# A fused attention and gated feed-forward kernel: the first q/k load cut in two, and a new order for every engine

## The chip, the cores and the metric

The kernel runs on one core of one Trainium2 chip. Its time is the device time of one execution in microseconds (us). Times of one instruction are given in nanoseconds (ns) where that is plainer. TensorE (PE in the rows) multiplies matrices, VectorE (DVE), ScalarE (ACT) and GpSimd (POOL) do the element-wise work, and SyncE (SP) issues the transfers.

## The reference, cut to what matters

Causal attention over 4 batches, 12 heads, 448 positions and 64 dimensions per head, and then a feed-forward part (768 to 1024 to 768) with a convolution of three taps over the positions and a gate:

```
scores = mask(q @ k.T / 8);  attn = softmax(scores);  x = attn @ v      # per head
h = relu(x @ w_in)                                                      # 768 -> 1024
c = conv_w[0]*h[s-1] + conv_w[1]*h[s] + conv_w[2]*h[s+1]
out = (h * sigmoid(c)) @ w_out                                          # 1024 -> 768
```

## The kernel before, in words

**Attention.** Two heads make a pair; there are 6 pairs in each of 4 batches, so 24 pairs, numbered g. For each pair SP loads `raw` (k and q, transposed, 128 partitions of 2 x 448 numbers) and `vraw` (the values). TensorE computes the scores (L453) in blocks of 64 queries. A block k needs keys 0 to 64(k+1) alone, and the blocks are taken in the order 6, 5, 1, 3, 4, 2, 0. For the first two batches the scores are two steps, (6, 5, 1) and (3, 4, 2, 0); for the last two they are one. VectorE adds the mask and finds the row maximum (L488), ScalarE takes the exponential and its sum (L494), TensorE transposes the result (L553), ScalarE or VectorE copies the transposes out of PSUM (L562), and TensorE multiplies them by the values (L583). In batch 0 the division by the sum comes last, and TensorE spreads the reciprocals over the rows (L599); in the others ScalarE or VectorE divides before the transposes (L525).

**Feed-forward.** Numbers are cut into a high and a low part (`parts`, `wih`, `wil`, `woh`, `wol`), and a product is three matmuls of 128 x 128 by 448 columns: L899 for `w_in` of batches 0 and 1, L779 for a joint form of batches 2 and 3 with sums of weights, L957 for `w_out`: 1116 in all. Between the two, `activate` does relu (L915), taps, gate and the cut into parts. The weights are loaded in 32 pieces of 384 columns (L361) and converted by a chain on ACT, DVE and POOL (L365, L368, L326/L325/L329, L340). The finished rows are stored by SP (L971).

**What sets the order.** Nothing is written in its final order. `plan.add` records steps: an engine (or several to choose from), a cost in ns, what the step needs and makes, and which buffers it takes and frees. `Plan.run` then goes through the open steps, always issues the one with the lowest rank, and moves that engine's clock on by the step's cost. A rank is the time at which the step could start, plus a lateness, plus a number from the table `OFFSET`. `SWITCH` is the cost that the planner adds when TensorE goes from one kind of step to another (0 products, 1 scores, 2 values, 3 transposes), and `FROM` the time at which it lets an engine begin. So each engine's order, and the choice between engines, comes out of these numbers; on the chip each engine runs its own list strictly in that order and waits on semaphores.

TensorE begins with eight matmuls on zeros (`idle`, L301), which write a bank that nothing reads, and two more such fills (4 and 7 matmuls) stand near the first pairs. PSUM's eight banks are three rings: `S` (four, for scores), `PT` (two, for transposes and values) and `acc` (two, for products).

Of the kernel before, what the change touches and what calls it, by code (L numbers as in the profile page):

```python
# [8 lines left out]
F32 = mybir.dt.float32  # L9
# [14 lines left out]
class Plan:  # L24
# [11 lines left out]
    FROM = {"PE": 3800.0, "SP": 500.0, "ACT": 3500.0}  # L36
    ISSUE = {}
    OFFSET = {
        "PT": {10: -100, 11: 250, 14: -500, 15: -11650, 18: -11650, 19: 200, 20: -150, 21: -100, 6: -7550},
        "after": {5: 9100},  # L40
        "c12": {0: 1950},
        "c22": {1: 550, 2: 6050, 3: 19800},
        "chain": {114: 6500, 142: 9650, 187: 20000, 197: 1800, 206: 7100, 215: 9600, 231: 7300, 29: 3150, 61: 7000},
        "cw": {0: 350},
        "exp": {0: -400, 1: 100, 11: 300, 12: 2650, 14: -100, 16: -6850, 17: -2150, 18: -18750, 20: -3000, 21: -8700, 22: -50,
            23: 450, 4: -9450, 5: 600},
        "g": {(0, 1): -250, (1, 1): 150, (1, 2): 300, (1, 5): -50, (1, 7): -50, (2, 1): -150, (2, 2): 200, (2, 3): 150, (3,
            1): -200, (3, 4): 9800, (3, 5): 16500},
        "least": {10: -450, 15: -2000, 16: -6900, 17: -500, 21: 450, 4: 150, 5: 150, 9: -250},
# [11 lines left out]
        "raw": {3: -12900, 4: 250, 5: 3750, 8: 550, 9: -1150},  # L61
        "rb": {1: -4300, 3: -15800},
        "s2": {1: 150, 2: -300, 3: -100},
        "s3": {0: -16000, 3: 100},
        "s4": {0: 150, 1: 100, 3: 14550},
        "scores": {16: -20000, 18: -14750, 4: 100, 5: 100, 6: -4750},
        "sum": {(1, 0): 950, (1, 1): -500, (1, 3): 150, (2, 2): -6650, (2, 3): -100, (3, 1): 1450, (3, 3): -6050},
        "t1": {2: -450},
        "t3": {0: -10350, 1: 150},
        "t4f": {0: 2700, 1: 450},  # L70
        "u2": {0: 700},
        "vraw": {1: 650, 2: 150, 22: 5000, 3: -850, 4: 3800, 5: 650, 7: 250},
# [4 lines left out]
    }  # L77
    SWITCH = {(0, 1): 90, (0, 2): 90, (3, 1): 90, (3, 2): 90, (1, 2): 95, (2, 1): 95, (1, 0): 200, (2, 0): 200, (1, 3): 100, (2, 3): 100, (0, 3): 20}
# [11 lines left out]
    def at(self, key):  # L90
        return self.slot[key]
# [119 lines left out]
def attn_ffn_kernel(ctx: ExitStack, tc: tile.TileContext, qk, v, w_in, conv_w, w_out, out):  # L211
# [8 lines left out]
    nc = tc.nc  # L220
    P = 128
# [11 lines left out]
    RANK = (6, 5, 1, 4, 3, 0, 2)  # L233

# [68 lines left out]
    def setup():  # L303
        nc.gpsimd.memset(bank_zeros, 0.0)
        idle(bank[7], 8)
# [105 lines left out]
    def pair(b, hp):  # L411
# [8 lines left out]
        def load():  # L420
            nc.sync.dma_start(out=at(raw), in_=qk[b, hp])

        def load_v():
            nc.sync.dma_start(out=at(vraw).rearrange("p c j d -> p c (j d)"), in_=v[b, hp])

        plan.add(
            "SP", 1130, load, needs=after, makes=[raw], late=0,
            take=[("xg" if near else "raw", raw, lambda pool: pool.tile([P, 2, S], F32, name="raw", tag="xg"))],
        )
# [17 lines left out]
        def scores(blocks):  # L447
            for k in blocks:
                s, o = place(k)
                for j in range(2):  # L450
                    t = at(raw)[half(j)]
                    for k0, k1, to in [(128, 192, o), (0, 128, o + 64)] if k == 2 else [(0, KEYS[k], o)]:
                        nc.tensor.matmul(  # L453
                            at(s)[half(j ^ (k in SWAPPED)), to : to + k1 - k0], lhsT=t[:, 1, 64 * k : 64 * k + 64],
                            rhs=t[:, 0, k0:k1], start=True, stop=True,
                        )
# [597 lines left out]
```

## Time and profile before

| | us |
|---|---|
| median of 3 runs (lowest, highest) | 374.61 (374.46, 375.0) |
| the profiled execution, its time | 374.62 |
| the profiled execution, its span | 372.8 |

The span goes from the first instruction to the last. The execution's time is 1.8 us longer, which lies around the span; the profiled execution is within 0.01 us of the median.

### The profile page before, as it was taken

How to read it: one execution, taken by the hardware profiler on the slowest of the kernel's cores; microseconds unless marked ns; L12 is line 12 of the kernel's file. 1: busy time of each engine (PE TensorE's matmuls, PEld its weight loads, DVE VectorE, ACT ScalarE, POOL GpSimd, SP SyncE). 2: the span in 40 equal slices, each digit the busy share in tenths (PEclk: the TensorE clock that was granted, in tenths of full speed). 3: DMA queues.
4: the chain of work that ended last, by engine and by line, in shares of the span. 5: the costliest groups of instructions: out<-in, count | busy, mean ns of one | idle time of the engine just before them, and what ended most of it. 6: DMA issues, size and time to landing. Idle time of an engine off the chain costs nothing.

```text
span 372.8 us, 8941 instructions
## 1 busy us (share of the span) xinstructions
PE 364.5 (98%) x3367; PEld 305.5 (82%) x3367; DVE 265.0 (71%) x739; ACT 258.9 (69%) x708; POOL 164.4 (44%) x201
## 2 busy tenths in 40 slices
PE   8999998999999899999999999999999999999996
PEld 4777776988888697898988887887899999999995
DVE  4788897977874837866896868558999897742500
ACT  4899899899999556886769866879656147523211
POOL 2067774466553220324348887861211822521400
PEclk9999999999999999999999999999999999999999
DMA  7996414325575332501122253120000000111011
GB/s 272 401 358 207 168 44 143 86 81 167 146 242 172 118 120 88 159 11 37 49 86 87 72 152 111 61 62 26 1 2 0 2 0 0 52 49 49 2 74 74
DMA packets 15162, 37.54 MB, mean 101 GB/s; under 512 B 1808, under 2 KB 4880, under 8 KB 15120
## 3 DMA queue, kind: packets, MB, share of 16 engines
q1 hardware_dynamic: 15120, 36.99, 29.8%
q8 instruction: 26, 0.43, 0.5%
q14 instruction: 16, 0.13, 0.1%
HBM read 31.47 MB, written 5.51 MB: 99 GB/s over the span
## 4 chain that ended last, share of the span: by engine, by line
PE 86%; ACT 5%; DVE 4%; issue 2%; DMA 1%; POOL 1%; SPq 0%; ACTq 0%; DVEq 0%; POOLq 0%
PE bank L957 30%; PE bank L899 14%; PE bank L779 11%; PE bank L553 10%; PE bank L583 10%; PE bank L453 9%; ACT p L494 2%; DMA wraw<-in_w_out_dram 1%; PE bank L599 1%; PE bank L301 1%; ACT p L525 1%; DVE u L676 1%; DVE top L676 1%; DVE keep L676 0%; ACT u L968 0%
## 5 line engine op out<-in xcount | busy, mean ns | idle before, releaser
L957 PE MATMUL bank<-parts,woh 128*128 128x448 f32 x384 | 113.9, 371 | 0.0
L494 ACT ACTIVATE p<-bank,negm 128x320 f32<-128x320 f32 (+6 forms) x168 | 78.1, 483 | 17.2 <-DVE negm L488 16.1
L957 PEld LDWEIGHTS bank<-parts,woh 128*128 128x128 f32 x384 | 71.5, 188 | 5.4
L488 DVE CUSTOM_DVE_ANT_0 bank<-bank,mask 128x384 f32<-128x384 f32 (+6 forms) x168 | 66.2, 454 | 11.4 <-PE bank L453 11.3
L957 PE MATMUL bank<-parts,wol 128*128 128x448 f32 x192 | 71.5, 372 | 0.0
L340 POOL TENSOR_TENSOR parts<-u,parts 128x448 fp32r<-128x448 f32 x38 | 45.9, 1212 | 39.5 <-ACT parts L325 38.0
L899 PE MATMUL bank<-parts,wih 128*128 128x448 f32 x192 | 57.2, 376 | 0.5 <-ACT hr L915 0.5
L922 DVE SCALAR_TENSOR_TENSOR u<-hr,cw,u 128x448 f32<-128x448 f32 x64 | 46.8, 739 | 9.6 <-ACT u L935 8.9
L553 PE MATMUL bank<-ident,p 128*128 128x128 f32 x336 | 51.0, 278 | 2.6 <-DVE u L646 1.3
L553 PEld LDWEIGHTS bank<-ident,p 128*128 128x128 f32 x336 | 38.4, 140 | 11.8 <-ACT parts L325 1.6
L453 PE MATMUL bank<-raw 64*64 64x128 f32 (+5 forms) x768 | 46.0, 359 | 0.0
L583 PEld LDWEIGHTS bank<-pt,vraw 64*64 64x64 f32 x960 | 30.8, 133 | 15.8 <-issue 7.4
L583 PE MATMUL bank<-pt,vraw 64*64 64x64 f32 (+3 forms) x960 | 43.2, 317 | 0.1
L779 PE MATMUL bank<-parts,wih 128*128 128x448 f32 x150 | 42.9, 367 | 0.3 <-DVE hr L810 0.3
L525 ACT ACTIVATE p<-p,rcp 128x448 f32<-128x448 f32 (+6 forms) x90 | 40.8, 511 | 1.6 <-DVE rcp L513 1.5
L562 ACT COPY pt<-bank 128x512 f32<-128x512 f32 (+1 forms) x61 | 32.5, 550 | 12.7 <-PE bank L553 11.9
L329 POOL TENSOR_SCALAR parts<-u 128x448 fp32r<-128x448 f32 x20 | 11.9, 597 | 66.2 <-DVE u L928 50.4
L453 PEld LDWEIGHTS bank<-raw 64*64 64x64 f32 x768 | 29.5, 134 | 13.9 <-issue 7.6
L899 PEld LDWEIGHTS bank<-parts,wih 128*128 128x128 f32 x192 | 34.8, 188 | 4.2 <-ACT hr L915 0.9
L957 PEld LDWEIGHTS bank<-parts,wol 128*128 128x128 f32 x192 | 36.1, 188 | 2.5
L899 PE MATMUL bank<-parts,wil 128*128 128x448 f32 x96 | 35.9, 374 | 0.0
L494 ACT ACTIVATION_READ_ACCUMULATOR p<-bank,negm 128x1 f32 x168 | 35.8, 213 | 0.0
(91 smaller groups left out, 544.1 us busy)
## 6 DMA issues: line engine op xcount, KB each, us to landing
raw<-in_qk_dram SPq DMA_DIRECT2D x24, 448.0 KB, 4.1
vraw<-in_v_dram SPq DMA_DIRECT2D x24, 320.0 KB, 3.6
wraw<-in_w_in_dram SPq DMA_DIRECT2D x16, 383.8 KB, 7.0
wraw<-in_w_out_dram SPq DMA_DIRECT2D x16, 383.8 KB, 3.2
out_dram<-u SPq DMA_DIRECT2D x24, 224.0 KB, 1.9
wraw<-in_conv_w_dram SPq DMA_DIRECT2D x1, 23.8 KB, 5.9
```

Source lines behind the costliest of these rows:

```text
L340: engine.tensor_tensor(out=out(), in0=src(), in1=f32(hi()), op=ALU.subtract)
L453: nc.tensor.matmul(at(s)[half(j ^ (k in SWAPPED)), to : to + k1 - k0], lhsT=t[:, 1, 64 * k : 64 * k + 64], rhs=t[:, 0, k0:k1], start=True, ...
L488: nc.vector.tensor_tensor_reduce(out=t, in0=t, in1=mask[:, S - 64 : S - 64 + n] if k == 2 else mask[:, S - n : S], scale=-0.125, scalar=3. ...
L494: nc.scalar.activation(at(t)[:, h : h + n], at(s)[:, o : o + n], AF.Exp, bias=negm[g % 2][:, c : c + 1], scale=-1.0, accum_out=ssum[g % 2] ...
L525: mul(t, t, rcp[g % 2][:, c : c + 1])
L553: nc.tensor.matmul(to, lhsT=p, rhs=ident, is_transpose=True)
L562: copy(at(part)[:, o : o + n], at(pt)[:, :n])
L583: nc.tensor.matmul(at((pv, r))[half(j), q0:q1], lhsT=at(vraw)[half(r), c if c < 3 else 3 + (c - 3) // 2, j], rhs=t[half(r), :, j], start=c ...
L779: nc.tensor.matmul(at(bank)[:, :S], lhsT=weights(w)[:, c], rhs=at(operands[c])[:, part], start=q == 0, stop=q == len(prods) - 1,)
L899: nc.tensor.matmul(at(ph)[:, :S], lhsT=block(w, NCC * f + cc), rhs=at(x)[:, part], start=q == 0, stop=q == len(prods) - 1)
L922: nc.vector.scalar_tensor_tensor(out=t, in0=src, scalar=w, in1=t, op0=ALU.mult, op1=ALU.add)
L957: nc.tensor.matmul(at(po)[:, :S], lhsT=block(w, NF * m + f), rhs=at(g)[:, part], start=q == 0, stop=q == len(prods) - 1)
```

## The change

It has four parts.

1. The queries of every pair lie in memory in the order 6, 5, 1, 3, 4, 2, 0, and the first pair's `raw` is loaded by two transfers: columns 0 to 640 (all keys and the queries of blocks 6, 5 and 1), then the other 256. The first score step needs the first of them alone. All other pairs are loaded in one transfer as before.
2. TensorE begins with five matmuls on zeros in place of eight.
3. The planner's costs of TensorE's steps, of the exponential and of relu are other numbers, the switches between kinds are other numbers, the values are a kind of their own (mode 2), and TensorE's start is 2900 in place of 3800.
4. Every entry of `OFFSET` is another.

The work is the same: as many score, transpose, value, spread and product matmuls, on as many columns.

```diff
-    FROM = {"PE": 3800.0, "SP": 500.0, "ACT": 3500.0}
+    FROM = {"PE": 2900.0, "SP": 500.0, "ACT": 3500.0}
...
-        "PT": {10: -100, 11: 250, 14: -500, 15: -11650, 18: -11650, 19: 200, 20: -150, 21: -100, 6: -7550},
+        "PT": {10: -50, 17: -250, 19: -100, 23: -50, 4: -150, 5: -350, 6: -400},
...
-    SWITCH = {(0, 1): 90, (0, 2): 90, (3, 1): 90, (3, 2): 90, (1, 2): 95, (2, 1): 95, (1, 0): 200, (2, 0): 200, (1, 3): 100, (2, 3): 100, (0, 3): 20}
+    SWITCH = {(0, 1): 178, (0, 2): 170, (0, 3): 85, (1, 0): 95, (1, 2): 10, (1, 3): 95, (2, 0): 213, (2, 1): 103, (2, 3): 110, (3, 1): 167, (3, 2): 167, (3, 3): 120}
...
+    QUERIES = (6, 5, 1, 3, 4, 2, 0)
+    FIRST = S + 64 * 3
...
-        idle(bank[7], 8)
+        idle(bank[7], 5)
...
-        plan.add(
-            "SP", 1130, load, needs=after, makes=[raw], late=0,
...
+        cuts = (0, FIRST, 2 * S) if g == 0 else (0, 2 * S)
+        for z in range(len(cuts) - 1):
+            plan.add(
+                "SP", 1130 if g else (300, 830)[z], lambda z=z: load(cuts[z], cuts[z + 1]), needs=after, makes=[raw, (raw, z)], late=0,
...
-                "PE", 1650, lambda: scores((6, 5, 1, 3, 4, 2, 0)), makes=[("scores", g, 0), ("scores", g, 1)], drop=[raw],
+                "PE", 1573, lambda: scores((6, 5, 1, 3, 4, 2, 0)), makes=[("scores", g, 0), ("scores", g, 1)], drop=[raw],
...
-                    "PE", 830, lambda blocks=blocks: scores(blocks), makes=[("scores", g, i)], drop=[raw], mode=1,
+                    "PE", (930, 870)[i] if g else (1500, 980)[i], lambda blocks=blocks: scores(blocks), makes=[("scores", g, i)], drop=[raw], mode=1,
...
-                    "ACT", 237 + 0.83 * n, expo, needs=[("least", g, s)] + ([("exp", ("p", g, home))] if h else []), early=84,
+                    "ACT", 245 + 0.83 * n, expo, needs=[("least", g, s)] + ([("exp", ("p", g, home))] if h else []), early=84,
...
-                "PE", 110 * n // P, transp, slack=SLACK if b else 0, mode=3,
+                "PE", 109.3 * n // P - 75, transp, slack=SLACK if b else 0, mode=3, early=-75,
...
-            "PE", 170, lambda: spread(0), needs=[("r1", g, 0)], makes=[("rb", g, 0)], mode=1, take=[("S", rb)]
+            "PE", 400, lambda: spread(0), needs=[("r1", g, 0)], makes=[("rb", g, 0)], mode=1, take=[("S", rb)]
...
-            "PE", 1800, product, needs=[("pt", g, 0), ("pt", g, 1), vraw, ("rb", g, 0)], makes=[(pv, 1)], mode=1,
+            "PE", 2073, product, needs=[("pt", g, 0), ("pt", g, 1), vraw, ("rb", g, 0)], makes=[(pv, 1)], mode=2,
...
-            "PE", 1560, times_v, needs=[("pt", g, 0), ("pt", g, 1), vraw, *gate], makes=[(pv, 1)], mode=1,
+            "PE", 1473, times_v, needs=[("pt", g, 0), ("pt", g, 1), vraw, *gate], makes=[(pv, 1)], mode=2,
...
-        plan.add("ACT", 436, relu, needs=needs, makes=[(hr, 1)], take=[] if ph == hr else [("hr", hr)], drop=[] if ph == hr else [ph], late=0)
+        plan.add("ACT", 480, relu, needs=needs, makes=[(hr, 1)], take=[] if ph == hr else [("hr", hr)], drop=[] if ph == hr else [ph], late=0)
...
-    qk = _np.stack([k, q], axis=2).transpose(0, 1, 4, 2, 3)
+    queries = _np.concatenate([q[:, :, 64 * n : 64 * n + 64] for n in (6, 5, 1, 3, 4, 2, 0)], axis=2)
+    qk = _np.stack([k, queries], axis=2).transpose(0, 1, 4, 2, 3)
```

All cost numbers in the diff are the planner's own; how long something takes on the chip stands in the rows further down. Lines of the changed kernel are three to seven further on (L453 is L459, L553 is L559, L583 is L589, L779 is L785, L361 is L364, L971 is L977).

**Three places in the order.** First, SP's queue at the very start, before:

```order
L421 DMA raw<-in_qk_dram 128x896 x2
L424 DMA vraw<-in_v_dram 128x640
L421 DMA raw<-in_qk_dram 128x896
L361 DMA wraw<-in_conv_w_dram 128x95
L424 DMA vraw<-in_v_dram 128x640
```

and in the changed kernel:

```order
L425 DMA raw<-in_qk_dram 128x640
L425 DMA raw<-in_qk_dram 128x256
L425 DMA raw<-in_qk_dram 128x896
L428 DMA vraw<-in_v_dram 128x640
L425 DMA raw<-in_qk_dram 128x896
L364 DMA wraw<-in_conv_w_dram 128x95
```

The first pair's 896 columns have become 640 and 256, and each later transfer stands one place further back.

Second, TensorE at the last transposes of the attention (L553, L559; `p` are the exponentials of the last pair), where only products of the joint form (L779, L785) remain to be done afterwards; before, from the last products ahead of them to the values product (L583):

```order
L779 MATMUL bank_142<-parts,wil_83 128x448
L553 MATMUL bank_140<-ident,p_1_235 128x128
L553 MATMUL bank_140<-ident,p_1_237 128x2x64
L553 MATMUL bank_140<-ident,p_0_238 128x2x64
L553 MATMUL bank_140<-ident,p_1_240 128x128
L553 MATMUL bank_139<-ident,p_1_233 128x2x64
L553 MATMUL bank_139<-ident,p_1_240 128x128
L553 MATMUL bank_139<-ident,p_1_235 128x128
L553 MATMUL bank_139<-ident,p_1_237 128x2x64
L553 MATMUL bank_140<-ident,p_1_240 128x128
L553 MATMUL bank_140<-ident,p_1_237 128x2x64
L583 MATMUL bank_139<-pt,vraw_230 64x384 x2
```

and in the changed kernel, after the four transposes of the first bank:

```order
L785 MATMUL bank_142<-parts,wil_84 128x448
L559 MATMUL bank_140<-ident,p_1_233 128x2x64
L559 MATMUL bank_140<-ident,p_1_240 128x128
L559 MATMUL bank_140<-ident,p_1_235 128x128
L559 MATMUL bank_140<-ident,p_1_237 128x2x64
L785 MATMUL bank_142<-parts,wih_68 128x448 x2
L559 MATMUL bank_139<-ident,p_1_240 128x128
L559 MATMUL bank_139<-ident,p_1_237 128x2x64
L785 MATMUL bank_142<-parts,wil_84 128x448
L785 MATMUL bank_141<-parts,wih_69 128x448 x2
L589 MATMUL bank_140<-pt,vraw_231 64x384 x2
```

The ten transposes in one piece have become four, four and two with one and two products between them, and three products stand between the last transposes and the values.

Third, SP's queue where the first finished rows are stored (`out_dram`) and the last pieces of `w_out` are still to be loaded, before:

```order
L971 DMA out_dram<-u_249 128x448
L361 DMA wraw<-in_w_out_dram 128x1535 x2
L421 DMA raw<-in_qk_dram 128x896
L424 DMA vraw_231<-in_v_dram 128x640
L361 DMA wraw<-in_w_out_dram 128x1535
L971 DMA out_dram<-u_249 128x448
L361 DMA wraw<-in_w_out_dram 128x1535
L424 DMA vraw_230<-in_v_dram 128x640
L421 DMA raw<-in_qk_dram 128x896
L361 DMA wraw<-in_w_out_dram 128x1535 x2
```

and in the changed kernel:

```order
L364 DMA wraw<-in_w_out_dram 128x1535
L425 DMA raw<-in_qk_dram 128x896
L364 DMA wraw<-in_w_out_dram 128x1535
L977 DMA out_dram<-u_249 128x448
L364 DMA wraw<-in_w_out_dram 128x1535 x2
L977 DMA out_dram<-u_249 128x448
L364 DMA wraw<-in_w_out_dram 128x1535 x2
```

Before, six of the sixteen pieces of `w_out` stand behind the first store and three of them behind the second; in the changed kernel four stand behind the first and two behind the second, and no load of a pair stands among them.

## Rows read from the trace of the kernel before

**Rows 1.** The page, part 1: busy us, share of the span, instructions.

```profile
PE 364.5 (98%) x3367; PEld 305.5 (82%) x3367; DVE 265.0 (71%) x739; ACT 258.9 (69%) x708; POOL 164.4 (44%) x201
```

**Rows 2.** Stretches: length, then PE, PEld, DVE, ACT, POOL busy, clock, DMA.

```profile
12.00:60.00 48.00, 47.03 (x717) 34.05 (x712) 39.77 (x135) 44.41 (x138) 30.11 (x36) 1.00 0.63 221
60.00:120.00 60.00, 59.76 (x571) 50.40 (x572) 45.75 (x126) 57.09 (x159) 32.34 (x38) 1.00 0.47 143
```

**Rows 3.** The chain of waits, its last long piece: start us, us, what.

```profile
310.94 58.38 PE bank L957 x288
```

**Rows 4.** Timeline of the start: start us, us, engine, line, instruction, idle before.

```profile
1.19 2.74 PE L301 MATMUL bank<-zeros 128*128 128x384 bf16 x8 [1.19 <-POOL zeros L304]
3.88 0.31 PEld L453 LDWEIGHTS bank<-raw 64*64 64x64 f32 x8 [0.64 <-DMA raw<-in_qk_dram]
5.69 0.57 DVE L488 CUSTOM_DVE_ANT_0 bank<-bank,mask 128x384 f32<-128x384 f32 x1 [3.97 <-PE bank L453]
7.02 0.63 ACT L494 ACTIVATE p<-bank,negm 128x448 f32<-128x448 f32 x1 [4.80 <-DVE negm L488]
7.08 0.82 PE L301 MATMUL bank<-zeros 128*128 128x384 bf16 x4
```

**Rows 5.** Transfers from 1 to 4.25 us: GB/s in 40 equal slices.

```profile
GB/s 0 0 0 0 0 0 0 0 132 132 221 88 176 132 265 176 221 309 353 309 397 353 397 397 397 441 397 397 309 397 353 353 353 265 441 265 397 441 265 485
```

**Rows 6.** Timeline of TensorE where kinds of work meet.

```profile
172.78 1.76 PE L583 MATMUL bank<-pt,vraw 64*64 64x384 f32 x40
174.36 1.74 PE L453 MATMUL bank<-raw 64*64 64x448 f32 x32
176.03 1.09 PE L553 MATMUL bank<-ident,p 128*128 128x128 f32 x8
...
252.06 1.76 PE L583 MATMUL bank<-pt,vraw 64*64 64x384 f32 x40
253.75 0.67 PE L957 MATMUL bank<-parts,woh 128*128 128x448 f32 x2
...
125.09 0.45 PE L957 MATMUL bank<-parts,woh 128*128 128x448 f32 x1
...
125.88 1.79 PE L453 MATMUL bank<-raw 64*64 64x448 f32 x32
```

**Rows 7.** Timeline of TensorE where a pair's scores come in two parts.

```profile
37.30 1.09 PE L453 MATMUL bank<-raw 64*64 64x448 f32 x12
38.33 1.09 PE L553 MATMUL bank<-ident,p 128*128 128x128 f32 x8
39.35 1.03 PE L453 MATMUL bank<-raw 64*64 64x256 f32 x20
40.32 0.47 PE L899 MATMUL bank<-parts,wih 128*128 128x448 f32 x1
```

**Rows 8.** Timeline of TensorE from 57 to 61 us.

```profile
57.44 0.45 PE L899 MATMUL bank<-parts,wil 128*128 128x448 f32 x1
...
58.97 0.69 PE L899 MATMUL bank<-parts,wih 128*128 128x448 f32 x2 [0.48 <-ACT hr L915]
...
60.24 0.66 PE L553 MATMUL bank<-ident,p 128*128 128x128 f32 x4 [0.39 <-ACT p L525]
```

**Rows 9.** Timeline of TensorE and VectorE from 120 to 124 us.

```profile
121.09 0.65 PE L957 MATMUL bank<-parts,woh 128*128 128x448 f32 x2
...
123.44 0.63 PE L553 MATMUL bank<-ident,p 128*128 128x128 f32 x4 [1.29 <-DVE u L646]
...
120.78 0.39 DVE L365 TENSOR_SCALAR top<-wraw 128x384 f16<-128x384 bf16 x1 [1.37 <-DMA wraw<-in_w_out_dram]
```

**Rows 10.** The chain of waits from 84 to 146 us: its one transfer.

```profile
115.75 5.01 DMA wraw<-in_w_out_dram
```

**Rows 11.** Timeline of TensorE at the last pair's transposes and values.

```profile
258.71 1.09 PE L553 MATMUL bank<-ident,p 128*128 128x128 f32 x8
...
260.53 2.15 PE L583 MATMUL bank<-pt,vraw 64*64 64x384 f32 x40
...
262.62 0.68 PE L779 MATMUL bank<-parts,wih 128*128 128x448 f32 x2
```

More of the change, by code (lines that the diff above doesn't have):

```diff
@@ new lines @@
+        "PT": {10: -50, 17: -250, 19: -100, 23: -50, 4: -150, 5: -350, 6: -400},
+        "c12": {0: 4800, 2: -1250},
+        "c21": {2: 300},
+        "c22": {2: 9550},
+        "chain": {10: 800, 103: 10100, 152: 4050, 187: 20000, 198: 1250, 215: 4100, 23: 1300, 231: 11950, 3: 1450, 34: 300,
+            36: 1250, 39: 2550, 69: 1700},
+        "exp": {11: 1050, 12: -9700, 14: -100, 16: -100, 18: 100, 2: -50, 20: -2550},
+        "g": {(0, 1): -200, (1, 3): 150, (1, 5): -100, (2, 0): -200, (2, 1): -150, (2, 3): 50, (2, 5): 50, (3, 2): 450, (3,
+            4): 16550, (3, 5): 18800, (3, 7): 19950},
@@ new lines @@
+        "least": {0: -250, 10: 1100, 13: 1200, 14: 1000, 15: -50, 17: -11000, 18: -450, 19: -650, 2: 150, 20: 1150, 21: -1200,
[10 rows of a table added]
+        "raw": {0: -700, 9: 2850},
+        "rb": {1: 2000, 2: -7300},
+        "s1": {0: -1850},
+        "s3": {0: -4750, 2: 350},
+        "s4": {3: 13350},
+        "scores": {10: 150, 11: 100, 13: 100, 3: -100, 5: -150, 6: -100, 7: -2600},
+        "sum": {(1, 2): -15350, (1, 3): 350, (2, 0): -17950, (2, 1): -100, (2, 2): -100, (3, 1): 1350, (3, 3): -500},
+        "t1": {0: 1250, 2: 150},
@@ new lines @@
+        "t1f": {1: 750},
+        "t3": {0: 1000, 2: 50},
+        "t3f": {1: 150, 2: -9550},
+        "t4": {0: 7450, 1: 6950, 2: 14650},
+        "t4f": {0: -20000, 2: 2100},
+        "u2": {1: -5400},
+        "vraw": {1: 250, 18: 950, 2: -20000, 21: -6200, 6: -8250, 9: 250},
+        "w": {(1, 10): 1450, (1, 12): -700, (1, 13): 900, (1, 14): 1850, (1, 15): 150, (1, 5): 50, (1, 6): 50, (1, 7): -150,
+            (1, 8): 1250},
+        "x": {1: -300, 13: 500, 16: -8800, 17: -13750, 21: 15500, 23: 3050, 4: -200, 8: 1250, 9: 1600},
@@ L418, in pair, with load @@
         after = [("p", g - (AHEAD if near else FAR))]
-        def load():
-            nc.sync.dma_start(out=at(raw), in_=qk[b, hp])
+        def load(c0=0, c1=2 * S):
+            to, of = at(raw).rearrange("p t s -> p (t s)"), qk[b, hp].rearrange("p t s -> p (t s)")
+            nc.sync.dma_start(out=to[:, c0:c1], in_=of[:, c0:c1])
         def load_v():
             nc.sync.dma_start(out=at(vraw).rearrange("p c j d -> p c (j d)"), in_=v[b, hp])
-        plan.add(
-            "SP", 1130, load, needs=after, makes=[raw], late=0,
-            take=[("xg" if near else "raw", raw, lambda pool: pool.tile([P, 2, S], F32, name="raw", tag="xg"))],
-        )
+        cuts = (0, FIRST, 2 * S) if g == 0 else (0, 2 * S)
+        for z in range(len(cuts) - 1):
+            plan.add(
+                "SP", 1130 if g else (300, 830)[z], lambda z=z: load(cuts[z], cuts[z + 1]), needs=after, makes=[raw, (raw, z)], late=0,
+                take=[] if z else [("xg" if near else "raw", raw, lambda pool: pool.tile([P, 2, S], F32, name="raw", tag="xg"))],
+            )
         plan.add(
@@ L453, in scores @@
                         nc.tensor.matmul(
-                            at(s)[half(j ^ (k in SWAPPED)), to : to + k1 - k0], lhsT=t[:, 1, 64 * k : 64 * k + 64],
+                            at(s)[half(j ^ (k in SWAPPED)), to : to + k1 - k0], lhsT=t[:, 1, 64 * QUERIES.index(k) : 64 * QUERIES.index(k) + 64],
                             rhs=t[:, 0, k0:k1], start=True, stop=True,
@@ L467, in pair @@
                 plan.add(
-                    "PE", 830, lambda blocks=blocks: scores(blocks), makes=[("scores", g, i)], drop=[raw], mode=1,
-                    needs=[raw, ("scores", g, 0) if i else ("norm", g - 2), (("pv", g - 3), 1), ("rb", g - 2, 0)], take=[(("S", "acc") if g < 4 else "S", ("S", g, 2 * i + z)) for z in range(2)],
+                    "PE", (930, 870)[i] if g else (1500, 980)[i], lambda blocks=blocks: scores(blocks), makes=[("scores", g, i)], drop=[raw], mode=1,
+                    needs=[raw if g or i else (raw, 0), ("scores", g, 0) if i else ("norm", g - 2), (("pv", g - 3), 1), ("rb", g - 2, 0)], take=[(("S", "acc") if g < 4 else "S", ("S", g, 2 * i + z)) for z in range(2)],
                 )
@@ L785, in link @@
             plan.add(
-                "PE", 204, prod,
+                "PE", 203.3, prod,
                 needs=[("chain", i) if i else ("unit", 1, NF + NM - 1), (operands[c], 0), (operands[c], 1), *(() if q else needs)],
@@ L903, in ffn1 @@
             plan.add(
-                "PE", 204, prod, needs=[(x, 0), (x, 1), ("w", 0, (NCC * f + cc) // 3), (ph, q) if q else before(b, f)],
+                "PE", 203.3, prod, needs=[(x, 0), (x, 1), ("w", 0, (NCC * f + cc) // 3), (ph, q) if q else before(b, f)],
                 makes=[(ph, q + 1)] + ([("unit", b, f)] if q == len(prods) - 1 else []), take=[("acc", ph)] if q == 0 else [],
@@ L961, in ffn2 @@
             plan.add(
-                "PE", 204, prod, needs=[(g, 0), (g, part), ("w", 1, (NF * m + f) // 3), (po, q) if q else before(b, NF + m)],
+                "PE", 203.3, prod, needs=[(g, 0), (g, part), ("w", 1, (NF * m + f) // 3), (po, q) if q else before(b, NF + m)],
                 makes=[(po, q + 1)] + ([("unit", b, NF + m)] if q == len(prods) - 1 else []), take=[("S" if b == B - 1 and m < 3 else "acc", po)] if q == 0 else [],
```

23 lines of the change are left out of this document (1 added, 22 removed), and 25 rows, old and new, of the table OFFSET.

## The prediction

> **What bounds the kernel now.** I read the page first: TensorE is busy for 98% of the span [rows 1], so a new order can win little by filling holes; it must shorten what TensorE does or waits for. A matmul's busy time holds its way through the array, though, so I go by the distance from one start to the next. A product costs 0.203 us by that (288 of them in 58.38 us [rows 3]), and 1116 are 226 us that no order changes. The chain of waits from 269 us on is products alone; nothing is to be had there. The table of stretches comes next: from 12 to 120 us ScalarE is nearly as full as TensorE, 44.41 of 48 us and 57.09 of 60 [rows 2], so in the first third TensorE waits for ScalarE, and later it does not. Then I looked in the timeline for places where TensorE's starts are further apart than the work between them needs. Three are large.
>
> At 57.44 us seven products stand until 60.24, 2.80 us; 7 x 0.203 and 0.09 for the change to transposes are 1.51, so 1.29 are lost. The named releasers are ScalarE's relu, which frees a bank, and its scaling of the exponentials [rows 8]: two steps stuck in ScalarE's full list. At 121.09 four products last until 123.44, 2.35 us for 0.90 of work: 1.45 lost. There TensorE waits for VectorE's addition (L646), which stands behind a weight conversion, which waited 1.37 us for a piece of `w_out` [rows 9]. That piece was issued at 115.75, right behind a store in SP's queue, and took 5.01 us to land [rows 10]. At 258.71 ten transposes last 1.82 us and the values after them 2.09 [rows 11]; eight transposes ahead of a 64 x 64 kind take 1.02 [rows 7], so ten take 1.27, and values ahead of a product 1.69 [rows 6], so 0.55 and 0.40 are lost, 0.95 together, since each bank must be copied out before it is filled again and nothing else was put between. The three are 3.7 us.
>
> **The cut load.** The first scores start at 3.88 us, when the first pair has landed, although TensorE was done with its zeros [rows 4]. VectorE and then ScalarE follow at 5.69 and 7.02, and with ScalarE the bound, what comes earlier here should shift the whole first third. The slices of the transfer rates are 0.081 us long [rows 5]. Added up from the first busy one, 458,752 bytes (the whole pair) are reached in the 20th of them and 327,680 (640 columns) in the 16th: 0.32 us. Bounds: nothing, if a packet takes its time whatever it holds; and if time goes with bytes from 1.65 to 3.88 us, 2/7 of 2.23, that is 0.64. I take 0.32, since those slices are the transfer itself. The other 256 columns are covered by the first score step, which takes over a microsecond. All later transfers are issued one place back; the second pair's scores follow the first pair's directly on TensorE, but VectorE has six maxima of the first pair to do in between, so I cost that at nothing; without that cover it would be one issue, some 0.4 us.
>
> **Three matmuls on zeros fewer.** They ran while nothing was there to do, so they cost and give nothing by themselves. Eight of them take 2.74 us, 0.32 each, which is 384 columns at the 1.2 GHz level; four at 7.08 take 0.16 each, the 2.4 GHz level [rows 4]. With five, TensorE is done at about 2.8 us and then waits some 0.7 us for the load. If the clock rises later for it, the first scores are slower: at 1.2 GHz the first step's two passes over 960 columns are 1.60 us, against about 1.35 now, and the second pair's scores would come some 0.6 us late for VectorE. So 0 to 0.6; I take 0 in the sum. By the Trainium skill, "TensorE: Matmul & The Clock Gate", Part 1, the clock is set by how busy TensorE has lately been, which speaks for a later rise here; by it the sum would be 0.3 to 0.6 us higher. The trace of before has no gap at this place and cannot tell.
>
> **The order of TensorE.** Scores, values and spreads use quarters of the array, products and transposes the whole. In the two built programs I counted how often such a group of quarter work stands between full work: 40 times before, 43 after. Values followed by scores take 174.36 - 172.78 = 1.58 us, values followed by a product 1.69, and three products ahead of scores take 0.79 in place of 0.61 [rows 6]: to part a group costs 0.11 + 0.18 = 0.29, three times 0.87. One more pair has its scores in two parts, 1.03 + 0.97 us [rows 7] against 1.67 in one [rows 6]: 0.33, of which 0.11 is in the 0.29 already, so 0.22. Together 1.09 us more work on an engine that is the bound. The kinds between which transposes and products alternate more often (61 to 75 times from transposes to products) I cost at nothing: the change of 0.09 is made up by the next start. Lower bound 0, if all of this falls into waits of the first third.
>
> **The waits.** What is late at 57 us is ScalarE. Counted up to the twelfth values product, which in both programs has the same matmuls ahead of it (229 products among them), ScalarE has five instructions fewer: 25 roundings for 32, and two others more. At up to 0.63 us [rows 4] that is some 2.7 us of the engine that was waited for, against about 1.1 more on VectorE. So I count the 1.29 as gone. At the last pair the order shows products between the transposes and ahead of the values: the 0.95 are gone too. The wait for `w_out` I leave: fewer pieces stand behind the stores, but still four. Bounds: all three gone, -3.7; none, 0.
>
> **Sum.** -0.32 + 1.09 - 1.29 - 0.95 = -1.47 us. From the profiled execution's 374.62, which is the median within 0.01, this gives 373.15: **373.1 us**.
>
> **Rivals.** *The waits only move.* ScalarE is full to 120 us [rows 2], so a place freed of one wait meets the next; then only the load's 0.32 and perhaps one of the waits are gained against 1.09: -0.32 + 1.09 - 0.95 = -0.2, 374.4 us. For it: three waits with three different causes sit in a program that was ordered by the same planner. Against it: ScalarE's shorter list.
>
> *The rest goes as well.* Without pair loads among the last pieces of `w_out` these share the transfer engines with less, and the 1.45 goes too: 373.1 - 1.45 = 371.7 us.
>
> *Slower: `w_out` behind the stores.* SP issues in order, a store waits for the last product of its rows, and pieces behind it are late by as much. Before, one such piece cost 1.45 us. In the changed kernel four stand behind two stores, two and two in a row. If three of the four hold an engine's list as the one did, that is 2.9 more: 373.15 + 2.9 = 376.0. It decides from two such waits on top of the one (one alone leaves 374.6). For it: 5.01 us from issue to landing is long against the products around it; against it: more pieces are loaded ahead of the first store (12 of 16, not 10), so those behind it may be needed later.
>
> *The clock.* Five zeros in place of eight put off the rise: 373.4 to 373.7 us, as above.
>
> **Chances.** The sum as it stands 0.36; the clock 0.08; the rest goes as well 0.14; the waits only move 0.17; slower by `w_out` or a new wait of its size 0.25. About 0.2% (0.75 us) is what a measurement of this kernel can tell from no change. So faster is 0.36 + 0.14 and most of the clock's 0.08: 0.56; same 0.18; slower 0.26. The forecast's own range is 372.2 to 373.9. To hold 8 in 10 it must reach both to 371.7, less half a microsecond of the load's bound, and to the slower case: 371.2 to 376.4.
>
> **What would show it.** The first score matmul at about 3.55 us and VectorE's first maximum 0.3 us earlier than 5.69; if it stands at 5.4 or later with the matmuls on columns at half rate, the clock. No product run near 57 us that lasts over a microsecond longer than its count times 0.203. Between the last pair's transposes no start further apart than the work, and values in 1.69. A VectorE or ScalarE conversion that waits for `w_out` between 95 and 125 us, and a TensorE gap behind it, is the slower rival. TensorE's groups should cost what rows 6 show; if a parted group costs much less, the new order is better than I say. I am wrong if new waits of a microsecond appear in the stretch from 60 to 255 us, where before has only the one.

## The result, and the profile after

| | before | after |
|---|---|---|
| median, us (lowest, highest, runs) | 374.67 (374.46, 375.0, 4) | 378.25 (377.06, 378.81, 4) |
| the profiled execution, time and span, us | 374.62, 372.8 | 378.81, 377.0 |

The ratio is 1.0094, with a 95% interval of 1.0073 to 1.0116: the change makes the kernel 3.6 us slower. The prediction was 373.1 us, with a range up to 376.4. Direction and range are both wrong. The profiled execution is the slowest of the four; what its profile shows is therefore more than the median's 3.6 us.

The page's part 1 of the changed kernel, as in [rows 1], and the two stretches of [rows 2] with the same columns:

```profile
PE 368.5 (98%) x3364; PEld 305.2 (81%) x3364; DVE 266.6 (71%) x739; ACT 260.9 (69%) x714; POOL 160.2 (42%) x195
```

```profile
12.00:60.00 48.00, 46.77 (x721) 34.18 (x720) 39.44 (x139) 44.52 (x138) 30.72 (x36) 1.00 0.65 228
60.00:120.00 60.00, 59.87 (x534) 48.94 (x533) 48.44 (x137) 57.36 (x159) 30.84 (x36) 1.00 0.46 140
```

The work is the same, and TensorE is busy for 4.0 us longer. Neither view tells where. So I counted matmuls: the 615th product is the first that has all of the attention ahead of it in both programs, and from there on TensorE has the same 502 products left and nothing else. These are start times from the timelines, in us:

| | first values product | product 615 | product 701 | product 731 | last product |
|---|---|---|---|---|---|
| before | 13.80 | 266.85 | 284.84 | 290.92 | 368.94 |
| after | 15.17 | 267.30 | 284.84 | 293.45 | 373.02 |
| difference, and its growth | +1.37 | +0.45 (-0.92) | 0.00 (-0.45) | +2.53 (+2.53) | +4.08 (+1.55) |

So 1.37 us are lost at the start; the new order wins all of it back by product 701; and 4.08 us are lost after that, in a stretch where nothing but products is left on TensorE.

The timeline of the start, to be read against [rows 4]: TensorE, then VectorE's first maximum, then ScalarE's first exponential.

```profile
1.19 1.78 PE L304 MATMUL bank<-zeros 128*128 128x384 bf16 x5 [1.19 <-POOL zeros L307]
3.73 4.97 PE L459 MATMUL bank<-raw 64*64 64x448 f32 x44 [0.76 <-DMA raw<-in_qk_dram]
8.64 1.37 PE L304 MATMUL bank<-zeros 128*128 128x384 bf16 x4
...
5.92 0.57 DVE L494 CUSTOM_DVE_ANT_0 bank<-bank,mask 128x384 f32<-128x384 f32 x1 [4.20 <-PE bank L459]
...
7.25 0.63 ACT L500 ACTIVATE p<-bank,negm 128x448 f32<-128x448 f32 x1 [5.03 <-DVE negm L494]
```

The scores start 0.15 us earlier than before, but their 44 matmuls hold TensorE from 3.73 to 8.64, 4.91 us, where before the next row starts 3.20 us after them (3.88 and 7.08). The four zeros behind them tell why: 1.37 us in place of the 0.82 of [rows 4], about 0.32 us each in place of 0.16, so TensorE is still at its 1.2 GHz level at 9 us. The granted clock of the profile reads 1.00 in this stretch all the same; the level is read from the steps. Ahead of the scores TensorE had stood idle for 0.76 us. By the Trainium skill, "TensorE: Matmul & The Clock Gate", Part 1: The HAM clock gate, "the default state is throttled, and activity releases the throttle"; the trace agrees: the first zeros go at 0.32 us each in both kernels, and those at 7.08 us before at 0.16.

Next, the places that the prediction named: near 57 us, near 121 us and the last pair's values. TensorE's timeline, against [rows 8, 9, 11]:

```profile
56.83 0.47 PE L905 MATMUL bank<-parts,wih 128*128 128x448 f32 x1
57.97 1.03 PE L459 MATMUL bank<-raw 64*64 64x256 f32 x20 [0.67 <-DVE u L625]
...
121.00 1.76 PE L589 MATMUL bank<-pt,vraw 64*64 64x384 f32 x40
122.69 0.67 PE L963 MATMUL bank<-parts,woh 128*128 128x448 f32 x2
...
265.62 1.76 PE L589 MATMUL bank<-pt,vraw 64*64 64x384 f32 x40
267.30 0.47 PE L785 MATMUL bank<-parts,wil 128*128 128x448 f32 x1
```

The wait for ScalarE is gone, but a product at 56.83 is followed only 1.14 us later, by scores that wait for VectorE. The 1.45 us at 121 are gone, and the last pair's values take 1.68 us, with no wait ahead of them.

Last, the end. TensorE, ScalarE and VectorE from 278 to 289 us:

```profile
285.04 0.37 PE L785 MATMUL bank<-parts,wil 128*128 128x448 f32 x1
286.84 0.68 PE L785 MATMUL bank<-parts,wih 128*128 128x448 f32 x2 [1.43 <-ACT wih L328]
287.70 0.47 PE L785 MATMUL bank<-parts,wil 128*128 128x448 f32 x1 [0.19 <-DVE wil L343]
...
284.87 0.51 ACT L328 CAST wih<-top 128x384 fp32r<-128x384 f32 x1 [1.63 <-DVE top L682]
286.27 0.51 ACT L328 CAST wih<-top 128x384 fp32r<-128x384 f32 x1 [0.89 <-DVE top L682]
...
278.84 2.47 DVE L928 SCALAR_TENSOR_TENSOR u<-hr,cw,u 128x448 f32<-128x448 f32 x4 [1.20 <-ACT u L941]
281.37 1.22 DVE L934 SCALAR_TENSOR_TENSOR u<-u,hr 128x448 f32<-128x448 f32 x2
282.62 1.27 DVE L343 TENSOR_TENSOR parts<-u,parts 128x448 fp32r<-128x448 f32 x2
283.81 0.55 DVE L682 TENSOR_TENSOR top<-wih,wih 128x384 f32<-128x384 f32 x1
284.28 1.02 DVE L682 TENSOR_TENSOR top<-top,wil 128x384 f32<-128x384 f32 x2
```

Product 703, at 286.84, wants a sum of weights. ScalarE rounds it at 286.27 and had waited for VectorE (L682), which got to the sums at 283.81 only, behind taps, gated products and parts of two units of batch 2 (L928, L934, L343). In the profile of before the sum that product 703 wants lies ahead of those steps, and the sum for product 712 between them. VectorE, then ScalarE:

```profile
268.59 0.97 DVE L676 TENSOR_TENSOR top<-wih,wih 128x384 f32<-128x384 f32 x1
269.60 1.99 DVE L676 TENSOR_TENSOR top<-top,wil 128x384 f32<-128x384 f32 x2
...
271.99 2.00 DVE L922 SCALAR_TENSOR_TENSOR u<-hr,cw,u 128x448 f32<-128x448 f32 x3
...
276.85 0.55 DVE L676 TENSOR_TENSOR top<-wih,wih 128x384 f32<-128x384 f32 x1
...
279.57 0.67 DVE L922 SCALAR_TENSOR_TENSOR u<-hr,cw,u 128x448 f32<-128x448 f32 x1
...
271.62 0.51 ACT L325 CAST wih<-top 128x384 fp32r<-128x384 f32 x1 [0.24 <-DVE top L676]
```

So before, VectorE began the first of these sums at 268.59, and ScalarE rounded it at 271.62, 13.6 us ahead of product 703 (285.25). The new order begins the same sum at 283.81, 15.2 us later.

And the chain of waits ends with the same 288 products as in [rows 3], at another length:

```profile
313.87 59.53 PE bank L963 x288
```

That is 59.53 us in place of 58.38, 206.7 ns from product to product in place of 202.7, with no wait in either. That is why 1.55 us are lost behind product 731 in this execution. The lowest of the changed kernel's four times, 377.06, lies 1.75 us below the profiled one, near to what the shorter distance would give (an estimate: 395 products at 4.0 ns are 1.58 us); it too is above the forecast's range.

### The profile page after: what moved, and what is told of

It reads as the page before. It is cut to its first block, busy times and chain, and to the rows that moved or that the text cites. A ratio compares the mean times of both kernels' runs of the same rounds, so it can differ in the third digit from the quotient of the medians.

```text
span 377.0 us, 8926 instructions
## 1 busy us (share of the span) xinstructions
PE 368.5 (98%) x3364; PEld 305.2 (81%) x3364; DVE 266.6 (71%) x739; ACT 260.9 (69%) x714; POOL 160.2 (42%) x195
## 4 chain that ended last, share of the span: by engine, by line
PE 82%; DVE 7%; ACT 4%; DMA 3%; POOL 2%; issue 2%; ACTq 0%; POOLq 0%; DVEq 0%
PE bank L963 30%; PE bank L905 14%; PE bank L785 10%; PE bank L459 9%; PE bank L559 9%; PE bank L589 8%; DVE u L928 1%; DMA wraw<-in_w_out_dram 1%; ACT p L500 1%; DVE bank L494 1%; DMA raw<-in_qk_dram 1%; DMA wraw<-in_w_in_dram 1%; PE bank L304 1%; DVE wraw L371 1%; ACT parts L328 1%
## 5 line engine op out<-in xcount | busy, mean ns | idle before, releaser
L500 ACT ACTIVATE p<-bank,negm 128x448 f32<-128x448 f32 (+6 forms) x168 | 78.3, 485 | 16.7 <-DVE negm L494 14.8
L905 PE MATMUL bank<-parts,wih 128*128 128x448 f32 x192 | 60.7, 384 | 0.0
L559 PE MATMUL bank<-ident,p 128*128 128x128 f32 x336 | 52.4, 277 | 0.4 <-ACT p L500 0.3
L928 DVE SCALAR_TENSOR_TENSOR u<-hr,cw,u 128x448 f32<-128x448 f32 x64 | 47.1, 754 | 5.6 <-ACT u L941 5.0
L459 PE MATMUL bank<-raw 64*64 64x128 f32 (+5 forms) x768 | 48.6, 372 | 1.6 <-DMA raw<-in_qk_dram 0.8
L559 PEld LDWEIGHTS bank<-ident,p 128*128 128x128 f32 x336 | 39.9, 141 | 9.5 <-issue 1.0
L343 POOL TENSOR_TENSOR parts<-u,parts 128x448 fp32r<-128x448 f32 x35 | 41.8, 1199 | 8.8 <-ACT parts L328 6.9
L785 PE MATMUL bank<-parts,wih 128*128 128x448 f32 x150 | 43.6, 370 | 1.4 <-ACT wih L328 1.4
L459 PEld LDWEIGHTS bank<-raw 64*64 64x64 f32 x768 | 30.3, 138 | 18.0 <-issue 8.4
L531 ACT ACTIVATE p<-p,rcp 128x256 f32<-128x256 f32 (+6 forms) x97 | 43.6, 509 | 1.2 <-DVE rcp L519 1.0
L568 ACT COPY pt<-bank 128x512 f32<-128x512 f32 (+1 forms) x68 | 36.1, 545 | 10.4 <-PE bank L559 9.3
L589 PE MATMUL bank<-pt,vraw 64*64 64x64 f32 (+3 forms) x960 | 42.9, 317 | 0.0
L589 PEld LDWEIGHTS bank<-pt,vraw 64*64 64x64 f32 x960 | 29.9, 133 | 15.9 <-issue 8.1
L332 POOL TENSOR_SCALAR parts<-u 128x448 fp32r<-128x448 f32 x23 | 14.4, 624 | 58.2 <-DVE u L934 44.9
```

The lines of the kernel that those rows point to most:

```text
L343: engine.tensor_tensor(out=out(), in0=src(), in1=f32(hi()), op=ALU.subtract)
L459: nc.tensor.matmul(at(s)[half(j ^ (k in SWAPPED)), to : to + k1 - k0], lhsT=t[:, 1, 64 * QUERIES.index(k) : 64 * QUERIES.index(k) + 64], r ...
L500: nc.scalar.activation(at(t)[:, h : h + n], at(s)[:, o : o + n], AF.Exp, bias=negm[g % 2][:, c : c + 1], scale=-1.0, accum_out=ssum[g % 2] ...
L531: mul(t, t, rcp[g % 2][:, c : c + 1])
L559: nc.tensor.matmul(to, lhsT=p, rhs=ident, is_transpose=True)
L568: copy(at(part)[:, o : o + n], at(pt)[:, :n])
```

## The experiments

Theory: three losses, apart from the order's own gain. The zeros left out put off the clock; VectorE's list makes TensorE wait at the weight sums; the last run of products goes at a longer distance. Rivals: the order hides the start; the sums wait for something else; the distance belongs to that stretch of the program. All kernels were run beside the kernel before; ratios are to it, with 95% intervals.

**The start: zeros and load.** Four kernels change one thing each. In the changed kernel:

```diff
-        idle(bank[7], 5)
+        idle(bank[7], 8)
```

> The changed kernel with eight matmuls on zeros in place of five, nothing else. Theory (the clock): in the changed kernel TensorE had 0.76 us without work ahead of its first score matmul, and the first 44 score matmuls then lasted 4.91 us against 3.20 us before; with eight zeros there is no such gap beyond that of before, the 44 matmuls take about 3.2 us again, and everything up to 260 us comes 1.2 to 1.4 us earlier, so the time falls from 378.2 to about 376.9 us. Rival (the order hides the start: TensorE waits for ScalarE and VectorE in the first third anyway): the start is faster, but the twelfth values product comes no earlier and the time stays within 0.4 us of the changed kernel's.

The changed kernel with one transfer for the first pair, and its five zeros:

```diff
-        cuts = (0, FIRST, 2 * S) if g == 0 else (0, 2 * S)
+        cuts = (0, 2 * S)
```

> The changed kernel with the first pair loaded in one transfer, five zeros kept. Theory (the load is worth little and its gap little more): the first score matmul starts about 0.15 us later than 3.73, the gap ahead of it grows by as much, the slow stretch stays, and the time is 0 to 0.3 us over the changed kernel's. Rival (the cut itself costs, since each later load stands one place further back): 0.3 us or more under the changed kernel.

The kernel before with five zeros:

```diff
-        idle(bank[7], 8)
+        idle(bank[7], 5)
```

> The kernel before with five matmuls on zeros in place of eight, its one transfer and its order kept. Theory (the clock): the gap ahead of the first score matmul becomes about 1 us, the first 44 score matmuls take about 4.9 us in place of 3.20, and the time rises from 374.7 by 1.0 to 1.5 us to about 376 us. Rival (hidden start): within 0.4 us of the kernel before. If this rises and the changed kernel with eight zeros doesn't fall, the order of the changed kernel hides what the order of before doesn't.

The kernel before with the change's first part alone, the queries' order and the cut load:

```diff
+        cuts = (0, FIRST, 2 * S) if g == 0 else (0, 2 * S)
```

> The kernel before with the first pair's load cut in two (and the queries' order in memory that it needs), eight zeros and the order kept. Theory: the first score matmul starts 0.15 us earlier, as in the changed kernel, the clock is that of before, and the time falls by 0.1 to 0.3 us, to about 374.5 us. Rival one (each later load one place back costs as much): no change within 0.1 us. Rival two (the second pair's load, later by an issue, stalls the second pair's scores): up by 0.3 us or more.

Later, the same with seven zeros:

```diff
-        idle(bank[7], 8)
+        idle(bank[7], 7)
```

> The kernel before with the cut load and seven zeros (with eight, TensorE's zeros ended at 3.86 us, after the first part had landed at about 3.73). Theory (the gap between zeros and scores is what put off the clock): the zeros end at about 3.5 us, TensorE waits some 0.2 us, the first score matmul starts at 3.73, and the first step of the scores takes as long as with eight zeros, so that the twelfth values product comes 0 to 0.15 us earlier; time within 0.2 us of the kernel with the cut and eight zeros. Rival (the number of zeros, the work done, is what counts): the first 44 score matmuls take over 4 us as with five zeros, and everything comes about 1 us later.

| | median, us | ratio | first values product | product 615 | last product |
|---|---|---|---|---|---|
| changed kernel, eight zeros | 376.99 | 1.0054 (1.0035 to 1.0074) | 13.58 | 265.46 | 371.21 |
| changed kernel, one transfer | 378.42 | 1.0099 (1.0076 to 1.0123) | 14.85 | 266.77 | 372.50 |
| before, five zeros | 374.98 | 1.0019 (0.9997 to 1.0040) | 14.74 | 267.25 | 369.35 |
| before, cut load | 374.62 | 1.0004 (0.9985 to 1.0023) | 13.31 | 265.54 | 367.69 |
| before, cut load, seven zeros | 374.81 | 1.0001 (0.9981 to 1.0021) | 14.10 | 267.01 | 369.15 |

TensorE's start in three of them, in the order of the table's rows one, three and five:

```profile
3.86 2.01 PE L459 MATMUL bank<-raw 64*64 64x448 f32 x32
6.37 1.09 PE L459 MATMUL bank<-raw 64*64 64x448 f32 x12 [0.50 <-DMA raw<-in_qk_dram]
7.40 0.82 PE L304 MATMUL bank<-zeros 128*128 128x384 bf16 x4
```

```profile
4.02 4.80 PE L453 MATMUL bank<-raw 64*64 64x448 f32 x44 [1.05 <-DMA raw<-in_qk_dram]
```

```profile
3.81 4.09 PE L458 MATMUL bank<-raw 64*64 64x448 f32 x44 [0.19 <-DMA raw<-in_qk_dram]
```

The clock is shown. With eight zeros in the changed kernel the 44 score matmuls hold TensorE for 3.54 us (3.86 to 7.40, 0.50 of it a wait) in place of 4.91, the zeros behind them take 0.16 us each again, the first values product comes 1.59 us earlier and product 615 1.84 (265.46 and 267.30). With five zeros the 44 are slow in the old order too. Over all profiles they take 3.16 to 3.78 us with eight zeros (eight profiles), 4.02 with seven, and 4.74 to 4.91 with five (three).

The rival, that the order hides the start, is out for the new order: its stretch from the first values product to product 615 takes 251.7 to 252.1 us in all seven profiles, wherever it starts. In the old order it isn't shown. With five zeros the first values product is 0.94 us later, and the transfer that TensorE waits for near 121 us [rows 9, 10] is issued 0.92 later (116.67 against 115.75), so nothing has been hidden up to there. That transfer then took 4.49 us in place of 5.01, and 0.40 us are left at product 615. In other profiles of the old order it took 4.14, 4.96 and 4.97 us, and TensorE's wait behind it was 0.41 to 1.29 us, so what came off lies in that transfer's own time, which varies from execution to execution, and no slack of the order is shown. In time, five zeros cost the old order 0.3 us in the median, which can't be told from nothing.

Seven zeros are a miss. The gap was only 0.19 us, as expected, but the 44 matmuls held TensorE for 4.02 us (3.81 to 7.83), over the 4 us of the rival, and the first values product came 0.79 us later than with eight. So the rival's condition is met, if by little: one profile with eight zeros and no gap reached 3.78. Product 615 came 1.47 later, but 0.82 of that is the wait near 121 us, 1.24 against 0.41.

The cut load is the smallest part. With eight zeros TensorE is busy with them until the scores begin at 3.86 to 3.88, cut or not, so nothing starts earlier on it, and the second part is then waited for (0.50 us). The first values product stands at 13.31 to 14.26 us in the five profiles with the cut and eight zeros and at 13.80 to 14.16 in the three with one transfer, and the clock rose at a different moment in these executions. In the times the cut can't be told from nothing: in the old order the ratio is 1.0004, with some 0.7 us to either side. With five zeros the cut kernel even is the later one in the profiles, 267.30 against 266.77 at product 615.

**The order alone.** The changed kernel with both edits above, one transfer and eight zeros: what is left is the new order.

> The change without its first two parts: the first pair in one transfer and eight zeros, as before, with the new order of all engines. Theory (the start lost 1.3 us and the end 3 us, and the order between them is worth about half a microsecond): the first values product stands 0.2 to 0.5 us later than with the cut load and eight zeros, TensorE waits again 1.4 us for the weight sums at about 285 us, and the time is 0 to 0.4 us over that kernel's 376.99, so 377.0 to 377.4 us. Rival (the order has a gain that the start hid): 375 us or less.

It took 375.61 us, ratio 1.0036 (1.0013 to 1.0058): between what the theory and the rival forecast. Product 615 stands at 265.94, 0.91 us before that of the kernel before, product 701 at 283.47, 1.37 before, and product 731 at 292.06, 1.14 behind. TensorE's wait (us in total, times, longest), and the two last pieces of the chain:

```profile
PE bank L785 <- ACT wih L328: 1.4, 1, 1.4
```

```profile
286.33 25.75 PE bank L785 x124
312.09 58.38 PE bank L963 x288
```

The wait is there. What I had missed is that the last 288 products can take 58.38 us in this order too; eleven of its twelve times lie below 376.2. One pair of profiles is not much: with eight zeros, product 701 stands at 283.58, 284.84 and 285.30 us in the three profiles of the old order and at 282.86 to 283.64 in the five of the new one, 1.4 earlier in the mean. The loss from there to product 731 hardly varies: 6.08 us in all five profiles of the old order, 8.59 to 8.65 in the six of the new one with all its instructions.

**The end: VectorE's list.** The changed kernel with eight zeros, without the six instructions ahead of the sums (so two units of batch 2 are not the reference's in this kernel and the next); everything else keeps its place:

```diff
         def tap(k):
+            if b == 2 and f in (2, 3) and k != 1:
+                return
...
         def gated():
+            if b == 2 and f in (2, 3):
+                return
```

> The changed kernel with eight zeros (376.99 us), in which six instructions are left out of VectorE's list: the outer taps and the gated product of the third and fourth unit of batch 2 (so these two units of the output are not those of the reference). They are the ones that stand ahead of the weight sums between 277.0 and 280.8 us; the lists of all other engines and the rest of VectorE's stay as they are. Theory (VectorE's list at the last weight sums is what TensorE waits for): the sums come some 3 us earlier, TensorE's waits of 1.45 us at 285 and 0.2 to 0.3 us at 286 to 288 are gone, and the time falls by 1.7 to 1.9 us to about 375.2. Second part (the products' distance is fixed by how their run begins, and the slow run of 395 began with the wait): with the wait the run that began at 266 us at 202.7 ns goes on at 202.7, and 395 x 4.0 ns = 1.6 us more are gained, to about 373.6 us. Rival (the sums wait for something else, a buffer or ScalarE): the wait stays above 1 us. Rival to the second part (the distance belongs to the instructions of that stretch): no wait, but 206.7 ns from about 285 us on, and about 375.2 us.

The same edit in the kernel before:

> The kernel before, in which the same six instructions are left out of VectorE's list as in the run with fewer taps (outer taps and gated product of two units of batch 2, so these two units aren't the reference's). Theory (before, VectorE was in time with the weight sums, because they stand between the taps and ahead of them): TensorE's only wait behind 263 us, 0.27 us at 268, stays, and the time stays within 0.2 us of the kernel before. Rival (VectorE bounds the end before as well, and the new order only shows it): the time falls by 0.5 us or more.

The first took 373.95 us, ratio 0.9987 (0.9969 to 1.0005); the second 374.30, 0.9997 (0.9975 to 1.0019). The last pieces of the first one's chain:

```profile
266.18 44.55 PE bank L785 x214
310.73 59.53 PE bank L967 x288
```

VectorE has gone from the chain: from 266 us on it is TensorE's products alone, and from product 702 to 703 it takes 0.21 us, where the changed kernel took 1.80. The sums came 2.0 us earlier against product 701 and not 3, since VectorE now waits for ScalarE in the step that stands ahead of them:

```profile
279.59 1.16 DVE L343 TENSOR_TENSOR parts<-u,parts 128x448 fp32r<-128x448 f32 x2 [3.16 <-ACT parts L328]
280.67 0.55 DVE L682 TENSOR_TENSOR top<-wih,wih 128x384 f32<-128x384 f32 x1
```

So VectorE is idle for 3.16 us with the sums behind that step in its list, though the kernel before began the first of them when TensorE stood at product 621: their place in the list delays them. A changed kernel with the sums moved forward and all work kept was not run. In the kernel before the same six instructions are worth nothing. So the first part of the theory holds: with the new order TensorE waits for VectorE at the sums, with the old one it does not. The second part does not hold as I put it: in this profile the products still fell out of step at a few waits of 0.1 us between 284 and 288 us, and the last run went at 206.7 ns. Its twelve times form two groups, nine from 373.5 to 374.0 and three from 375.2 to 375.6; the profiled execution, 375.64, is of the upper. The gap between the groups fits 395 x 4.0 ns = 1.58 us; that the lower group has the shorter distance is argued from that, not profiled.

**The distance between products.** A matmul of zeros ahead of each of the last eleven chains, in the changed kernel with eight zeros:

```diff
             def prod(q=q, f=f, w=w, part=part, g=g):
+                if b >= 2 and q == 0 and (b, m) > (2, 0):
+                    nc.tensor.matmul(bank[4][:, :128], lhsT=bank_zeros[:, :P], rhs=bank_zeros[:, :128], start=True, stop=True)
```

> The changed kernel with eight zeros (376.99 us), with one matmul of zeros on 128 columns put ahead of each of the last eleven chains of 24 products, so that the last long run of products, 395 at 206.7 ns, is broken into pieces of 24 from about 317 us on. Theory (each run takes one of two distances as it begins, 202.7 or 206.7 ns, and keeps it): the pieces show either, most of them 202.7 as in the rest of the kernel (83 of 102 runs of ten or more products in six profiles), so about nine of eleven pieces gain 24 x 4.0 ns = 0.1 us each, 0.85 us, against eleven zeros at 0.05 to 0.15 us each, 0.6 to 1.6 us: the time is 0.3 us lower to 0.8 us higher. Rival (the distance belongs to this stretch, by its buffers or its instructions): all pieces at 206.7 ns, and the time 0.6 to 1.6 us higher.

And one matmul of zeros, ahead of the first product of the last 288 alone (`(b, m, q) == (2, 0, 0)`); there the bank still held a sum of the joint form, so part of the output is not the reference's:

> The changed kernel with eight zeros and one matmul of zeros on 128 columns, ahead of the product at about 315 us with which the w_out part of batch 2 begins; the last run of 395 products falls into 131 and 264. Theory (the distance of 202.7 or 206.7 ns is taken where a run begins and kept to its end, and the same products can have either): the times of the single runs lie in up to four groups, 0, 0.5, 1.1 and 1.6 us above the fastest, and the profiled run has each of the two pieces at one distance throughout; cost of the restart itself about 0.1 us. Rival (the distance belongs to the stretch): both pieces at the same distance in every run, so two groups 1.6 us apart as without the restart.

The first took 377.81 us, ratio 1.0079 (1.0052 to 1.0106); the second 377.05, 1.0066 (1.0041 to 1.0091). From the end of the first one's chain:

```profile
285.88 25.74 PE bank L785 x124
...
316.56 4.91 PE bank L965 x24
321.54 4.92 PE bank L965 x24
...
361.78 5.01 PE bank L965 x24
366.86 5.02 PE bank L965 x24
```

With eight zeros and no restarts the first of these pieces is the same 124 products at the same place, and its row is

```profile
285.88 26.19 PE bank L785 x124
```

So the rival, that the distance belongs to the stretch, is out here: the same instructions at the same time take 25.74 us in one execution and 26.19 in another, and within one execution pieces of 24 take 4.91 or 5.02. A piece that has begun at one distance keeps it. (Not all pieces are of 24 products, as I had put it; behind 341 us some chains alternate, and there are three of 12 and one of 60.) But the pieces are not drawn one by one, as I had put it: the first ones in a row are short, the last ones in a row long. The restarts cost more than they gave. The single restart does not settle more: both of its pieces were at 206.7 ns in the profile, and its eight times, 375.83 to 377.69, show no clear groups.

## Why the prediction was wrong

- **The failed step: "The chain of waits from 269 us on is products alone; nothing is to be had there."** I read this as a stretch that no order changes, and did not look at VectorE's and ScalarE's new lists in it. The change had moved the weight sums there behind the steps of two units: the one that product 703 wants begins at 283.81 us in place of 268.59. The stretch between products 701 and 731 is 2.5 us longer for it, more than the order had gained until then; without the six instructions ahead of the sums 2.0 of them are gone (283.64 to 290.31, against 283.00 to 291.65). My slower rival had the right form, an engine's list held up and TensorE behind it, but the wrong place: no conversion of `w_out` holds TensorE in the changed kernel. My sign of being wrong looked from 60 to 255 us, and the new wait stood at 285.
- **"A product costs 0.203 us ... that no order changes."** It is 202.7 or 206.7 ns, and the last run of 395 was at the longer one: 1.6 us. All five profiles with the old order end at the shorter one; of those with the new order only the order alone does, and the restarts in part. So the longer one is not bound to the new order, and whether the change makes it more frequent is open. In other executions either order may have the other, as the groups in the times suggest.
- **"Three matmuls on zeros fewer ... I take 0 in the sum."** The rival of the clock came true and was bounded too low: 1.84 us at product 615 against 0.6 (one other profile with eight zeros and the cut load, that with fewer taps, has 1.19, as its clock rose later). I had counted only the first step's passes at the lower level; the second pair's scores and the zeros behind them ran at it too.
- **The cut load, -0.32.** With eight zeros the scores started at 3.86 to 3.88 us with the cut and without, so the term had nothing to act on. VectorE's first maximum came at 5.20 to 6.05 us in the five profiles with the cut and at 5.69 to 6.05 in the three without; in time nothing can be measured.
- **The order of TensorE and the waits, +1.09 - 1.29 - 0.95 = -1.15.** The order alone came to 1.37 us less by product 701, so the sum was about right, but partly by luck, for its parts were not. The last pair's 0.95 are gone as forecast. Of the 1.29 at 57 us about 0.75 came back as a wait for VectorE (1.14 us for a product and a change of kind), as the rival of waits that move has it. The 1.45 at 121 us, which I left standing, went; in the old order TensorE's wait there is itself 0.41 to 1.29 us in five profiles. The named waits with before's 0.27 at 268 us are 3.2 us less, so parted groups and new small waits cost some 1.8 us, not 1.09; I have not taken these apart.

Together, on the profiled executions: +1.37 at the start, -1.37 up to product 701, +2.53 at the sums and +1.55 by the distance are 4.08 of the 4.19 us. The last of the four differs from execution to execution and has no cause shown; the others do. No version here beats the kernel before measurably: the cut load alone and the cut load with seven zeros equal it.

## What to carry to other kernels

A stretch in which TensorE shows only products is not safe from a new order: look at what the other engines have to deliver in it, and by which product. Work that only keeps TensorE busy ahead of its first real matmuls is not free to remove; cost it by the rows at the lower clock level, for all that follows until the clock rises. Compare two orders at equal counts of work, not at equal times: only that showed that a gain had been made and was lost again.

## What the runs showed of the hardware that was not expected

A product of 128 x 128 by 448 columns (its operands are fp32r where VectorE and ScalarE write them; TensorE's rows say f32) has two distances to the next, 202.7 and 206.7 ns, and the last long run of products stays at one of them from its first few to its last in every profile that doesn't break it. What decides it is open. It isn't the place alone, since the same 124 products took 25.74 and 26.19 us; but it isn't free of the place either: the run of 24 near 218 us is at the longer one in all seven profiles of the new order. By the distance alone single times of one kernel could differ by up to 2 us (an estimate: 494 products from 269 us on before, 395 after, at 4.0 ns).

The granted clock in the profile's rows reads 1.00 in all stretches of the start, in every kernel, also where zeros of 384 columns take 0.32 us each, the 1.2 GHz level; only the steps tell. And the moment of the rise differs between executions that do the same up to there: in the changed kernel with eight zeros the first values product stood at 13.58 us, in the variants that differ from it only behind 260 us at 13.60, 13.71 and 14.26.
